# A chunked state-space scan and a feed-forward pair on one core: PSUM banks as tensors of their own, single-head outputs, dense tokens, another order of lead-in and weight decode

## The chip, the cores and the metric

The kernel runs on one core of a Trainium2 chip. The metric is device time in microseconds (us), the median of several executions; lower is better. Profiles come from one execution each. Names of engines: PE is the TensorE matmul, PEld its weight load, DVE the VectorE, ACT the ScalarE, POOL the GpSimd, SP the SyncE, whose queue issues nearly all DMAs here.

## What is computed

The reference, cut to what matters (4 batches, 8 heads, 768 tokens, head size 32, state size 16; feed-forward 256 to 2048 to 256):

```python
log_a = np.log(np.clip(a, 1e-06, 1.0))
for c in range(nc):                                   # chunks of tokens
    cum = np.cumsum(la, axis=-1)
    L = np.exp(cum[..., :, None] - cum[..., None, :]) * causal
    M = np.einsum('bhin,bhjn->bhij', Cc, Bc) * L
    y[:, :, sl] = M @ xc + (Cc @ state) * np.exp(cum)[..., None]
    state = exp(sum(la)) * state + sum_j(Bc_j xc_j * exp(cum_last - cum_j))
h = x @ w_in                                          # x: the scan's y, 3072 x 256
out = np.maximum(0.01 * h, h) @ w_out
```

The weights come in as 64-bit floats and are decoded on the chip.

## The kernel before

**Scan.** 12 chunks (`NC`) of 64 tokens (`Q`). Heads go in 4 pairs (`NG`), so 16 pairs of a head pair and a batch (`GB`). In each chunk PE does `states` (B by x into the state, 16 products), `scores` (C by B, 16), `decays` (exponents of L, 2), `outputs` (16 products of C and the old state, then 16 of the weighted scores and x) and `passed` (4). A 32-bit product is two matmuls with a weight load each. `spread_b` makes a block form of B (`bbd`) on DVE, `weigh` multiplies scores by decays on DVE, `weigh_b`, `weigh_c` and `end_decay` run on POOL, `decay_exp`, `passed_exp` and `keep_out` on ACT. Tokens lie block-diagonally in `xbd`: the two heads of a pair on 64 partitions each, with zeros beside them, so that one product of 128 by 64 serves both heads.

**Queues.** The order is written by hand, and every engine runs its instructions in that order. SP's queue carries the input chunks (`fetch_b`, `fetch_x`), the decay rows (`send_rows` to `dr`, `send_cols` to `dl`) and the raw weights (`fetch_w`). A wait is set between instructions that use the same tile.

**PSUM.** Four tiles `PS[0]` to `PS[3]` of two banks each serve the whole kernel. In the feed-forward `HB` is the two halves of `PS[0]` and of `PS[1]`, and `acc(t, m)` is half `m` of `PS[2 + t % 2]`.

**Feed-forward, first part.** Six stretches of 512 tokens (t = 0 to 5). For t = 0 and 1 there are 32 steps s: for hidden block f = s // 2 and t = s % 2, six matmuls of 128x128 by 128x512 (`products`: three for each half of the 256 inputs, since operands are split in a high and a low part) into `HB[s % 4]`; ACT makes `gh` and the activation in place, DVE the low part `gl`; two steps later (`LAG`) `ffn_out` issues six matmuls that add into `acc`. Between them run the decode jobs of the later blocks, three after each step: `dec_abs` (ACT), `dec_clamp`, `dec_shift`, `dec_sign`, `dec_low` (DVE), `dec_high` (ACT) and `dec_rest` (POOL), and for each pair of blocks `sum_weights` (POOL, ACT, POOL). In the last 24 steps `token_forms` are added.

**Feed-forward, second part.** The tokens of t = 2, 3 and then of t = 4, 5 go by a seven-product scheme: 8 blocks for each pair, 16 in all. A block is 21 matmuls into A, B, C, E (the four `HB`), of which A, B and C are written twice, and 24 matmuls of `ffn_out` by `run_out`. After A's first product ACT copies it (`act.copy(a, A)`), and DVE adds B to it. `store(t)` copies the two halves of `acc` out by ACT and DVE into `obs[m]` and sends them.

The second part begins as follows in each block:

```python
products(A, w_in(f0, 0), x(0), True, True)
act.copy(a, A)
products(B, sw(1), x(4), True, True)
dve.tensor_tensor(out=u2, in0=B, in1=a, op=ALU.add)
products(C, sw(0), x(3), True, True)
products(E, sw(2), x(5), True, True)
```

Of the kernel before, what the change touches and what calls it, by code (L numbers as in the profile page):

```python
# [45 lines left out]
def scan_ffn(ctx: ExitStack, tc: tile.TileContext, a_l, bcn_l, x_l, w_l, out_l):  # L46
# [10 lines left out]
    psum = open_pool(ctx, "psum", space=PSUM)  # L57

    PS = [psum.tile([128, 2, TS], F32, name=f"ps{i}") for i in range(4)]
# [4 lines left out]
    idle = base.tile([128, TS], BF16, name="idle")  # L64
# [67 lines left out]
    scan = ExitStack()  # L132
    cst = open_pool(scan, "cst", side="right")
# [3 lines left out]

    la = cst.tile([128, NC * GB], F32, name="la")
# [12 lines left out]
    xbd = [cst.tile([128, 2, GB * D], F32, name=f"xbd{i}") for i in range(4)]  # L151

    bcn, bbd, bnd, lts, es, cds, ss, tmps = ({} for _ in range(8))
# [12 lines left out]
    dve.memset(idle, 0.0)  # L166
    act.preload_act_table_set("natural_log_exp_and_others")
# [4 lines left out]

    sp.dma_start(la, a_l)
    fetch_b(0)
    fetch_x(0)
    keep_warm(PS[2][:, 0], WARM)

    dve.memset(later, 0.0)
    dve.memset(blk, 0.0)
    for hp in range(2):  # L180
        dve.memset(blk[64 * hp:64 * hp + 64, hp], 1.0)
    dve.memset(sign[:, :2], 1.0)
    dve.memset(sign[:, 2:], -1.0)
    pool.affine_select(
        out=later, in_=later, pattern=[[1, Q]], compare_op=ALU.is_ge, fill=-32768.0, base=0,
        channel_multiplier=-1,
    )
    pool.affine_select(
        out=upto, in_=blk, pattern=[[64, 2], [1, Q]], compare_op=ALU.is_ge, fill=0.0, base=0,
        channel_multiplier=-1,  # L190
    )
    pool.affine_select(
        out=after, in_=blk, pattern=[[-64, 2], [-1, Q]], compare_op=ALU.is_gt, fill=0.0, base=0,
        channel_multiplier=1,
    )
# [8 lines left out]
    dve.tensor_copy(  # L204
        dl[:64, :, 0], upto[:64, 0].unsqueeze(1).to_broadcast([64, NC, Q])
    )
    dve.tensor_copy(
        dl[:64, :, 1], upto[:64, 0].unsqueeze(1).to_broadcast([64, NC, Q])
    )
    dve.tensor_copy(dr[:64, 0], later.unsqueeze(1).to_broadcast([64, GB, Q]))  # L210
# [3 lines left out]
    act.copy(  # L214
        dl[64:KD, 0], sign[64:KD, :2].unsqueeze(2).to_broadcast([KD - 64, 2, Q])
    )
    dve.tensor_copy(dl[64:KD, 1:], dl[64:KD, :1].to_broadcast([KD - 64, NC - 1, 2, Q]))
    dve.tensor_tensor(out=seen, in0=upto[:, 0], in1=upto[:, 1], op=ALU.add)

    halves = [slice(0, GB // 2), slice(GB // 2, GB)]  # L220
    for h in range(2):
        pe.matmul(
            PS[0][:, h].rearrange("p (g i) -> p g i", i=Q), lhsT=dl[:64, 0],
            rhs=later.unsqueeze(1).to_broadcast([64, GB // 2, Q]), start=True, stop=True,
        )
# [4 lines left out]
    def fill_reach(h, eng):  # L230
        eng.tensor_tensor(
            out=reach[:, halves[h]],
            in0=la[:, halves[h]].unsqueeze(2).to_broadcast([128, GB // 2, Q]),
            in1=seen.unsqueeze(1).to_broadcast([128, GB // 2, Q]), op=ALU.mult,
        )

    prow = PS[3][:, 0].rearrange("p (a i) -> p a i", i=2 * Q)
    pcol = PS[3][:, 1, :NC * GB]
    flat = upto.rearrange("p h i -> p (h i)")
    pe.matmul(prow[:, 0], lhsT=la[:, :128], rhs=flat, start=True, stop=True)  # L240
    pe.matmul(prow[:64, 1], lhsT=la[:, 128:], rhs=flat, start=True, stop=True)
    fill_reach(0, pool)
    fill_reach(1, dve)
# [24 lines left out]
    def fill_slots(lo, hi):  # L268
        dve.tensor_copy(dr[:KD, lo:hi], dr[:KD, :1].to_broadcast([KD, hi - lo, GB, Q]))

    fill_slots(1, 4)
    split(0, 128)
    send_rows(1, 4, (0, 1, 2, 3, 4, 5), sp)
    send_cols(1)
    pe.matmul(
        pcol, lhsT=after.rearrange("p h i -> p (h i)"), rhs=la, start=True, stop=True
    )
    for h in range(2):
        pe.matmul(
            PS[0][:, h].rearrange("p (g i) -> p g i", i=Q),  # L280
            lhsT=after.rearrange("p h i -> p (h i)"), rhs=reach[:, halves[h]],
            start=False, stop=True, skip_group_check=True,
        )
# [39 lines left out]
    for i in range(4):  # L323
        for hp in range(2):
            p = slice(64 * hp, 64 * hp + 64)
            (dve if i == 0 else pool).memset(xbd[i][p, 1 - hp], 0.0)
    spread_b(0)

    def split_x(c):
        return xbd[c % 4].rearrange("p h (d g) -> p (h d) g", g=GB)  # L330

    def scores(c):
        for b in range(NB):
            for g in range(NG):
                r = slice(32 * g, 32 * g + 32)
                pe.matmul(
                    PS[1 + g // 2][:, g % 2, b * Q:(b + 1) * Q], lhsT=bbd[c][r, b].rearrange("p h i -> p (h i)"),
                    rhs=bcn[c][r, CT + b * Q:CT + (b + 1) * Q], start=True, stop=True,
                )

    def weigh(c, half):
        m = lts[c][:, 8 * half:8 * half + 8].rearrange("p (g b) i -> p g (b i)", g=2)
        dve.tensor_tensor(out=m, in0=PS[1 + half][:, :, :CT], in1=m, op=ALU.mult)

    zspace = PS[1][:, 1, CT:]
    espace = PS[3][:, 1, CT:]

    def states(c):
        x = split_x(c)
        for b in range(NB):  # L350
            for g in range(NG):
                gb = g * NB + b
                pe.matmul(
                    zspace[32 * g:32 * g + 32, b * 64:(b + 1) * 64], lhsT=bnd[c][:, gb].rearrange("p h n -> p (h n)"),
                    rhs=x[:, :, gb], start=True, stop=True, skip_group_check=True,
                )

    def keep_state(c):
# [49 lines left out]
    def outputs(c):  # L408
        x, mt = split_x(c), lts[c]

        def place(g, b):
            o = 64 * (g % 2)
            return PS[3][o:o + 64, g // 2, b * Q:(b + 1) * Q]

        if c:
            for b in range(NB):
                for g in range(NG):
                    r = slice(32 * g, 32 * g + 32)
                    pe.matmul(
                        place(g, b), lhsT=ss[c - 1][r, b * 64:(b + 1) * 64],  # L420
# [3 lines left out]
        for b in range(NB):  # L424
            for g in range(NG):
                gb = g * NB + b
                pe.matmul(
                    place(g, b), lhsT=x[:, :, gb], rhs=mt[:, gb], start=(c == 0 and b == 0),
                    stop=True, skip_group_check=True,
                )  # L430

    def keep_out(c):
        t, o = divmod(c, 2)
        cols = slice(o * CT, (o + 1) * CT)
        y = PS[3][:, :, :CT]
# [5 lines left out]
    def low_out(c):  # L441
        t, o = divmod(c, 2)
        cols = slice(o * CT, (o + 1) * CT)
        if t < 2:
            dve.tensor_tensor(
                out=xl[t][:, :, cols], in0=PS[3][:, :, :CT], in1=xh[t][:, :, cols],
# [3 lines left out]
    work = collections.deque()  # L450
    for f in range(EARLY_F):
        for g in (dec_abs, dec_clamp, dec_shift, dec_sign, dec_low):
            work.append((g, f))
        work.append((dec_rest, f))

    def background(n):
        for _ in range(n):
            if work:
                g, f = work.popleft()
                g(f)  # L460
                if g is dec_low:
                    dec_high(f)

    fetch_b(1)
    fetch_x(1)
    send_cols(2)
    for c in range(NC + 1):
        if 1 <= c < NC:
            states(c - 1)
        if c < NC:  # L470
            scores(c)
        if 1 <= c < NC:
            keep_state(c - 1)
        if c < NC:
            weigh(c, 0)
            weigh(c, 1)
            if c < NC - 1:
                weigh_b(c)
        if c + 1 < NC:
            decays(c + 1)  # L480
            decay_exp(c + 1)
        if c >= 1:
            outputs(c - 1)
        if c + 1 < NC:
            passed(c + 1)
        if c >= 1:
# [22 lines left out]
        if c >= 4:  # L509
            background(2)  # L510
    background(99)
# [12 lines left out]
    HB = [PS[0][:, 0], PS[0][:, 1], PS[1][:, 0], PS[1][:, 1]]  # L524

    def acc(t, m):
        return PS[2 + t % 2][:, m]
# [29 lines left out]
    def store(t):  # L557
        for m in range(2):
            ob = obs[m]
# [3 lines left out]
    obs = [mid.tile([128, TS], F32, name=f"ob{m}") for m in range(2)]  # L563


    def sum_weights(p):
# [3 lines left out]
        for o, x, y, op in (  # L570
# [39 lines left out]
    jobs = collections.deque()  # L610
    summed = 0
    for f in range(EARLY_F, NF):
# [152 lines left out]
```

## Time and profile before

| | |
|---|---|
| median of 3 runs | 425.88 us (425.29 to 426.62) |
| the profiled execution | 425.0 us |
| its span, first to last instruction | 423.3 us |
| PE busy, share of the span | 352.7 us, 83% |
| DVE, ACT, POOL busy | 210.2, 177.2, 86.0 us |
| mean granted TensorE clock | 0.945 of full speed |

The profile is of one core. A busy PE means that a matmul is in its pipeline, and not that it runs at its peak; matmuls overlap, so the step from one matmul's start to the next tells more than its duration. Idle time that is shown ahead of an instruction names the engine or transfer that ended it.

### The profile page before, as it was taken

To read this page: it belongs to the slowest core of one execution; us is meant where nothing else is said; L and a number is where in the kernel's file an instruction comes from. 1 tells how busy PE (TensorE), PEld (TensorE's weight loads), DVE (VectorE), ACT (ScalarE), POOL (GpSimd) and SP (SyncE) were. 2 spreads that over 40 slices of the span, in tenths; PEclk is the share of its full clock that TensorE was granted. 3 is DMA by queue.
4 is the path that set the end of the run, shared out by engine and by line. 5 is a ranking of instruction groups with operands and counts; after the bars stand their busy time and mean duration, and the time that the engine had idled before them with its cause. 6 is when DMAs were issued, how large, how long until landed. Compare 5 with 4: busy or idle time off the path is not lost.

```text
span 423.3 us, 6595 instructions
## 1 busy us (share of the span) xinstructions
PE 352.7 (83%) x2662; PEld 269.8 (64%) x2662; DVE 210.2 (50%) x352; ACT 177.2 (42%) x309; POOL 86.0 (20%) x114
## 2 busy tenths in 40 slices
PE   5849999976979787676669699999999799999994
PEld 2437888755757555454446477777777677777783
DVE  7624656433644545433333556666555555455551
ACT  2303433334544553433223555455444344444441
POOL 5422444413253442423123010000000000000000
PEclk8868999999998898979889899999999999999998
DMA  2256483103112111110000200000000200000002
GB/s 72 69 138 211 131 260 114 53 0 101 50 50 98 53 50 50 50 50 2 0 0 0 99 2 0 1 2 0 0 2 0 100 2 0 1 2 0 0 2 99
DMA packets 9902, 20.19 MB, mean 48 GB/s; under 512 B 3088, under 2 KB 3216, under 8 KB 9872
## 3 DMA queue, kind: packets, MB, share of 16 engines
q1 hardware_dynamic: 9872, 19.77, 14.3%
q8 instruction: 21, 0.34, 0.3%
q14 instruction: 9, 0.07, 0.0%
HBM read 16.35 MB, written 3.15 MB: 46 GB/s over the span
## 4 chain that ended last, share of the span: by engine, by line
PE 49%; ACT 11%; DVE 6%; POOL 5%; issue 4%; DMA 1%; ACTq 0%; DVEq 0%
PE ps L532 49%; POOL wtmp L576 2%; POOL wlb L127 2%; ACT gh L629 2%; ACT tmp L693 2%; ACT ps L630 2%; DVE gl L631 2%; DMA out_l<-ob 1%; DVE w L117 1%; ACT whb L124 1%; DVE w L111 1%; ACT gh L676 1%; ACT ob L560 1%; ACT w L97 1%; POOL wla L127 1%
## 5 line engine op out<-in xcount | busy, mean ns | idle before, releaser
L631 DVE TENSOR_TENSOR gl<-ps,gh 128x512 fp32r<-128x512 f32 x32 | 22.1, 690 | 78.3 <-ACT ps L630 78.3
L676 ACT ACTIVATE gh<-tmp 128x512 fp32r<-128x512 f32 x48 | 30.1, 628 | 67.0 <-DVE tmp L700 63.9
L532 PE MATMUL ps<-gh,whb 128*128 128x512 f32 x120 | 49.0, 408 | 0.0
L532 PE MATMUL ps<-gh,wlb 128*128 128x512 f32 x120 | 48.9, 408 | 0.0
L532 PE MATMUL ps<-gl,whb 128*128 128x512 f32 x120 | 48.5, 404 | 0.0
L678 DVE TENSOR_TENSOR gl<-tmp,gh 128x512 fp32r<-128x512 f32 x48 | 33.2, 692 | 20.6 <-ACT tmp L677 20.6
L532 PE MATMUL ps<-oph,wsh 128*128 128x512 f32 x64 | 27.6, 432 | 14.3 <-ACT tmp L693 14.3
L629 ACT ACTIVATE gh<-ps 128x512 fp32r<-128x512 f32 x32 | 19.0, 594 | 44.4 <-PE ps L532 43.3
L532 PE MATMUL ps<-xh,whb 128*128 128x512 f32 x40 | 18.3, 459 | 21.2 <-DVE gl L631 12.3
L677 ACT ACTIVATE tmp<-tmp 128x512 f32<-128x512 f32 x48 | 30.4, 632 | 1.5
L695 DVE TENSOR_TENSOR tmp<-ps,tmp 128x512 f32<-128x512 f32 x16 | 11.1, 692 | 37.8 <-PE ps L532 37.8
L532 PE MATMUL ps<-gh,wla 128*128 128x512 f32 x72 | 29.0, 402 | 0.0
L532 PE MATMUL ps<-gh,wha 128*128 128x512 f32 x72 | 28.8, 400 | 0.0
L532 PE MATMUL ps<-gl,wha 128*128 128x512 f32 x72 | 28.8, 400 | 0.0
L532 PEld LDWEIGHTS ps<-gh,whb 128*128 128x128 f32 x120 | 23.9, 199 | 5.7
L532 PEld LDWEIGHTS ps<-oph,wsh 128*128 128x128 f32 x64 | 12.4, 194 | 23.5 <-ACT tmp L693 21.2
L532 PEld LDWEIGHTS ps<-gh,wlb 128*128 128x128 f32 x120 | 23.8, 198 | 5.6
L532 PEld LDWEIGHTS ps<-gl,whb 128*128 128x128 f32 x120 | 23.7, 197 | 5.4
L532 PEld LDWEIGHTS ps<-xh,whb 128*128 128x128 f32 x40 | 8.4, 211 | 28.5 <-DVE gl L631 15.8
L532 PE MATMUL ps<-opl,wsh 128*128 128x512 f32 x64 | 25.7, 402 | 0.0
L532 PE MATMUL ps<-oph,wsl 128*128 128x512 f32 x64 | 25.7, 401 | 0.0
L127 POOL TENSOR_TENSOR wlb<-w,whb 128x512 fp32r<-128x512 f32 x10 | 12.7, 1275 | 63.5 <-ACT whb L124 63.5
(136 smaller groups left out, 722.7 us busy)
## 6 DMA issues: line engine op xcount, KB each, us to landing
raw<-w_l SPq DMA_DIRECT2D x16, 512.0 KB, 3.3
bcn<-bcn_l SPq DMA_DIRECT2D x12, 384.0 KB, 4.2
xbd<-x_l SPq DMA_DIRECT2D x24, 128.0 KB, 3.9
out_l<-ob SPq DMA_DIRECT2D x12, 256.0 KB, 2.0
dr<-parts SPq DMA_DIRECT2D x12, 8.0 KB, 1.9
dl<-parts SPq DMA_DIRECT2D x11, 12.0 KB, 3.8
la<-a_l SPq DMA_DIRECT2D x1, 96.0 KB, 1.9
dr<-parts SPq DMA_DIRECT2D x6, 6.0 KB, 1.8
```

The costliest lines, as they stand in the source:

```text
L97: act.activation(w32(f), raws[f][..., 1].bitcast(F32), AF.Abs)
L127: (eng or dve).tensor_tensor(out=weight(1, f), in0=w32(f), in1=weight(0, f), op=ALU.subtract)
L532: pe.matmul(space, lhsT=w, rhs=x, start=start and i == 0, stop=stop and i == 2, skip_group_check=again,)
L576: pool.tensor_tensor(out=o, in0=x, in1=y, op=op)
L629: act.activation(gh, hp, AF.Prelu, alpha=0.01)
L630: act.activation(hp, hp, AF.Prelu, alpha=0.01)
L631: dve.tensor_tensor(out=gl, in0=hp, in1=gh, op=ALU.subtract)
L676: act.activation(gh, v, AF.Prelu, alpha=0.01)
L677: act.activation(v, v, AF.Prelu, alpha=0.01)
L678: return g, lambda: dve.tensor_tensor(out=gl, in0=v, in1=gh, op=ALU.subtract)
L693: act.copy(a, A)
L695: dve.tensor_tensor(out=u2, in0=B, in1=a, op=ALU.add)
```

## The change

Six things are done.

1. In the feed-forward each of the eight PSUM banks is a tile of its own: `HB` four tiles, `ACC` four tiles. In the scan there are still four tiles of two banks (`pd`, `pa`, `pb`, `py`); `espace` moves from the tile of the outputs to that of the scores.
2. Tokens are dense (`xs`, one DMA for each chunk in place of two, and no zeros to set). `states` has 32 moving columns in place of 64, and `keep_state` does the block form by two DVE instructions with a mask. The second half of `outputs` is 32 products of 64 rows by 32 columns, one for each head and batch, in place of 16 of 128 by 64.
3. In the chunk loop `passed` and `passed_exp` go one chunk earlier.
4. The lead-in is in another order: `send_rows(1, 2)` ahead of the rest, two of its six DMAs on ACT's queue, fewer rows of `dl` to fill, four more warming matmuls.
5. The decode is placed step by step: `duty` in the scan, `plan` in the first part of the feed-forward, where block f's jobs lie in steps 2f-5 to 2f-1, and the forms come from step 4 on.
6. `obs` has four buffers, the fourth in `wtmp`.

```diff
-    PS = [psum.tile([128, 2, TS], F32, name=f"ps{i}") for i in range(4)]
+    pd, pa, pb, py = (psum.tile([128, 2, TS], F32, name=n) for n in ("pd", "pa", "pb", "py"))
...
-            for hp in range(2):
-                p = slice(64 * hp, 64 * hp + 64)
-                sp.dma_start(xbd[c % 4][p, hp], x_l[c, p])
+            xs[c] = pin.tile([128, GB, D], F32, name="xs")
+            sp.dma_start(xs[c].rearrange("p g d -> p (g d)"), x_l[c])
...
-    fill_slots(1, 4)
+    fill_reach(0)
     split(0, 128)
-    send_rows(1, 4, (0, 1, 2, 3, 4, 5), sp)
+    send_rows(1, 2, range(0, 4), sp)
+    send_rows(1, 2, range(4, 6), act)
     send_cols(1)
+    fill_reach(1)
+    fill_slots(2, 4)
...
         for b in range(NB):
-            for g in range(NG):
+            for h in range(NH):
+                g, hp = divmod(h, 2)
+                r = slice(64 * hp, 64 * hp + 64)
+                o = 32 * (h % 4)
                 gb = g * NB + b
                 pe.matmul(
-                    place(g, b), lhsT=x[:, :, gb], rhs=mt[:, gb], start=(c == 0 and b == 0),
-                    stop=True, skip_group_check=True,
+                    py[o:o + 32, h // 4, b * Q:(b + 1) * Q], lhsT=xs[c][r, gb], rhs=mt[r, gb],
+                    start=(c == 0 and b == 0), stop=True, skip_group_check=True,
                 )
...
     fetch_b(1)
     fetch_x(1)
+    send_rows(2, 4, range(6), sp)
     send_cols(2)
     for c in range(NC + 1):
+        if c + 1 < NC:
+            passed(c + 1)
...
         if c == 0:
             split(1, 64)
             fill_slots(4, 8)
+        if c == 1:
             send_rows(4, 8, range(6), sp)
...
-    HB = [PS[0][:, 0], PS[0][:, 1], PS[1][:, 0], PS[1][:, 1]]
+    HB = [psum.tile([128, TS], F32, name=f"h{i}") for i in range(4)]
+    ACC = [psum.tile([128, TS], F32, name=f"o{i}") for i in range(4)]
...
-            ob = obs[m]
+            ob = obs[t % 2 * 2 + m]
...
+    for f in range(NF):
+        o = 2 * (f - EARLY_F)
+        if f >= EARLY_F:
+            at(o - 1, dec_abs, f)
+            at(o, dec_clamp, f)
+            at(o, dec_shift, f)
+            at(o + 1, dec_sign, f)
+            at(o + 1, dec_low, f)
+            at(o + 2, dec_high, f)
+            at(o + 3, dec_rest, f, pool)
```

PE in the first part of the feed-forward, block f = 6, before: the end of one step's `ffn_out` and the products of t = 1 (`ps_61` is `PS[0]`, of which t = 0 has the other half).

```order
L532 MATMUL ps_63<-gh_1315,wha 128x512
L532 MATMUL ps_63<-gh_1315,wla 128x512
L532 MATMUL ps_63<-gl_1316,wha 128x512
L532 MATMUL ps_61<-xh_82,whb 128x512 [waits DVE_49]
L532 MATMUL ps_61<-xh_82,wlb 128x512
```

The same place now (`h_1529` is the second `HB`, `o_1533` and `o_1534` are `ACC`):

```order
L526 MATMUL o_1533<-gl_1519,wha 128x512
L526 MATMUL h_1529<-xh_74,whb 128x512
L526 MATMUL h_1529<-xh_74,wlb 128x512
L526 MATMUL h_1529<-xl_76,whb 128x512
L526 MATMUL h_1529<-xh_74,whb 128x512
L526 MATMUL h_1529<-xh_74,wlb 128x512
L526 MATMUL h_1529<-xl_76,whb 128x512
L526 MATMUL o_1534<-gh_1520,wha 128x512 [waits Activation_49]
```

The order is the same; the wait for DVE ahead of t = 1's products is gone, and the sums into `ACC` wait for their own `gh` and `gl`, which belong to two steps earlier.

PE in the second part, the start of a block, before (A and B are the halves of `ps_61`, C and E of `ps_62`):

```order
L532 MATMUL ps_61<-oph_1309,whb 128x512 [waits DVE_49]
L532 MATMUL ps_61<-oph_1309,wlb 128x512
L532 MATMUL ps_61<-opl_1310,whb 128x512
L532 MATMUL ps_61<-oph_1309,wsh 128x512 [waits Activation_49]
L532 MATMUL ps_61<-oph_1309,wsl 128x512
```

The same place now, from B's first product to A's second:

```order
L526 MATMUL h_1529<-oph_1512,wsh 128x512
L526 MATMUL h_1529<-oph_1512,wsl 128x512
L526 MATMUL h_1529<-opl_1513,wsh 128x512
L526 MATMUL h_1530<-oph_1512,wsh 128x512 [waits DVE_49]
L526 MATMUL h_1530<-oph_1512,wsl 128x512
L526 MATMUL h_1530<-opl_1513,wsh 128x512
L526 MATMUL h_1531<-oph_1512,wsh 128x512
L526 MATMUL h_1531<-oph_1512,wsl 128x512
L526 MATMUL h_1531<-opl_1513,wsh 128x512
L526 MATMUL h_1529<-oph_1512,whb 128x512 [waits DVE_49]
L526 MATMUL h_1529<-oph_1512,wlb 128x512
L526 MATMUL h_1529<-opl_1513,whb 128x512
```

B's first product no longer waits for ACT's copy of A; that wait now stands ahead of A's second product, which follows these rows, and B's second product waits for the DVE sum that has read B.

SP's queue in the lead-in, before (`dr` rows of slots 1 to 3, then of slots 4 to 7; `bcn` are the chunks of B and C):

```order
L256 DMA dr<-parts_109 1x48x64 x6
L263 DMA dl<-parts_109 48x1x128
L158 DMA bcn<-bcn_l 128x768
L164 DMA xbd_114<-x_l 64x512 x2
L263 DMA dl<-parts_109 48x1x128
L256 DMA dr<-parts_109 1x64x64 x6
L158 DMA bcn<-bcn_l 128x768
```

The same queue now:

```order
L251 DMA dr<-parts_109 1x16x64 x4
L258 DMA dl<-parts_109 48x1x128
L156 DMA bcn<-bcn_l 128x768
L161 DMA xs<-x_l 128x512
L251 DMA dr<-parts_109 1x32x64 x6
L258 DMA dl<-parts_109 48x1x128
L156 DMA bcn<-bcn_l 128x768
L161 DMA xs<-x_l 128x512
L258 DMA dl<-parts_109 48x1x128
L251 DMA dr<-parts_109 1x64x64 x6
L156 DMA bcn<-bcn_l 128x768
```

The input of chunk 2 (the third `bcn`) stood behind the six rows of slots 4 to 7, which wait for a split and a fill on DVE; it now stands ahead of them, behind six rows of slots 2 and 3, and it is chunk 3's input that follows the rows of slots 4 to 7.

## Rows read from the trace of the kernel before

**Rows 1.** Busy time by stretch: us, PE, PEld, DVE, ACT, POOL, clock, DMA

```profile
35.78:78.82 43.04, 43.04 (x1076) 35.48 (x1073) 24.90 (x53) 17.29 (x28) 19.84 (x24) 1.00 0.54 168
...
86.79:227.10 140.31, 103.91 (x375) 76.20 (x374) 59.10 (x95) 58.89 (x108) 47.10 (x56) 0.91 0.12 42
227.10:416.10 189.00, 173.81 (x727) 136.05 (x727) 103.98 (x156) 89.64 (x156) 3.18 (x3) 0.99 0.03 12
416.10:423.30 7.20, 1.36 (x6) 0.76 (x4) 1.38 (x2) 1.17 (x2) 0.00 (x0) 0.82 0.40 146
```

**Rows 2.** Waits from 86.79 to 227.1 us: total us, times, longest us

```profile
PE ps L532 <- DVE gl L631: 22.4, 14, 3.5
...
PE ps L532 <- ACT whb L124: 8.9, 5, 2.5
...
PE ps L532 <- POOL wlb L127: 5.1, 6, 0.9
```

**Rows 3.** Waits of the whole span, same columns

```profile
PE ps L532 <- ACT tmp L693: 14.3, 16, 2.6
```

**Rows 4.** Timeline of one step of the first part: start us, us, engine, line, operation

```profile
147.71 0.40 PE L532 MATMUL ps<-xh,whb 128*128 128x512 f32 x1
...
149.37 0.60 ACT L629 ACTIVATE gh<-ps 128x512 fp32r<-128x512 f32 x1 [2.10 <-PE ps L532]
...
149.87 0.59 ACT L630 ACTIVATE ps<-ps 128x512 f32<-128x512 f32 x1
...
150.27 0.40 PE L532 MATMUL ps<-gl,whb 128*128 128x512 f32 x1
150.49 0.69 DVE L631 TENSOR_TENSOR gl<-ps,gh 128x512 fp32r<-128x512 f32 x1 [1.69 <-ACT ps L630]
...
151.24 0.50 PE L532 MATMUL ps<-xh,whb 128*128 128x512 f32 x1 [0.57 <-DVE gl L631]
```

**Rows 5.** Timeline of the second part: a block's copy, its products, a stall between blocks

```profile
236.52 0.49 PE L532 MATMUL ps<-oph,wha 128*128 128x512 f32 x1 [0.87 <-DVE gl L678]
...
275.09 0.58 ACT L693 COPY tmp<-ps 128x512 f32<-128x512 f32 x1 [1.41 <-PE ps L532]
...
275.73 0.50 PE L532 MATMUL ps<-oph,wsh 128*128 128x512 f32 x1 [0.68 <-ACT tmp L693]
...
276.07 0.40 PE L532 MATMUL ps<-oph,wsl 128*128 128x512 f32 x1
...
285.93 0.40 PE L532 MATMUL ps<-opl,whb 128*128 128x512 f32 x1
```

**Rows 6.** Timeline of PE in one chunk of the scan

```profile
46.54 1.07 PE L353 MATMUL ps<-xbd,bnd 128*32 128x64 f32 x32
...
49.13 0.69 PE L419 MATMUL ps<-cd,ss 32*64 32x64 f32 x32
...
49.76 2.00 PE L427 MATMUL ps<-lt,xbd 128*64 128x64 f32 x32
...
51.92 0.30 PE L353 MATMUL ps<-xbd,bnd 128*32 128x64 f32 x4
```

**Rows 7.** Timeline of the lead-in and chunks 2 and 3

```profile
6.93 1.75 DVE L269 COPY dr<-dr 118x3072 bf16<-118x3072 bf16 x1
...
21.00 3.73 SPq L256 DMA_DIRECT2D dr<-parts  x6
...
24.77 0.58 SPq L158 DMA_DIRECT2D bcn<-bcn_l  x1
...
29.69 1.99 PE L336 MATMUL ps<-bcn,bbd 32*128 32x64 f32 x32 [6.28 <-DVE bbd L301]
...
36.78 1.12 PE L336 MATMUL ps<-bcn,bbd 32*128 32x64 f32 x32
```

**Rows 8.** Timeline of the end

```profile
417.06 0.40 PE L532 MATMUL ps<-gl,whb 128*128 128x512 f32 x1
...
419.58 0.69 DVE L560 COPY ob<-ps 128x512 f32<-128x512 f32 x1 [2.17 <-ACT ob L560]
```

**Rows 9.** Group by line, 35.78 to 78.82 us: busy us, mean ns of one

```profile
L427 PE MATMUL ps<-lt,xbd 128*64 128x64 f32 x256 | 16.0, 278 | 0.0
```

More of the change, by code (lines that the diff above doesn't have):

```diff
@@ L132, in scan_ffn @@
     scan = ExitStack()
+    psum = open_pool(scan, "psum", space=PSUM)
+    pd, pa, pb, py = (psum.tile([128, 2, TS], F32, name=n) for n in ("pd", "pa", "pb", "py"))
     cst = open_pool(scan, "cst", side="right")
@@ L136, in scan_ffn @@
     p3 = open_pool(scan, "p3", bufs=3, side="right")
+    idle = cst.tile([128, TS], BF16, name="idle")
     la = cst.tile([128, NC * GB], F32, name="la")
@@ L150, in scan_ffn @@
     reach = cst.tile([128, GB, Q], F32, name="reach")
-    xbd = [cst.tile([128, 2, GB * D], F32, name=f"xbd{i}") for i in range(4)]
-    bcn, bbd, bnd, lts, es, cds, ss, tmps = ({} for _ in range(8))
+    bcn, xs, bbd, bnd, lts, es, cds, ss, tmps = ({} for _ in range(9))
     def fetch_b(c):
@@ L181, in scan_ffn @@
         dve.memset(blk[64 * hp:64 * hp + 64, hp], 1.0)
[L182 to L195, printed above, removed]
+    dve.memset(later, 0.0)
+    keep_warm(pa[:, 0], WARM)
     pool.affine_select(
@@ L228, in scan_ffn, with fill_reach @@
     act.activation(la, la, AF.Ln)
-    def fill_reach(h, eng):
-        eng.tensor_tensor(
+    dve.tensor_tensor(out=seen, in0=upto[:, 0], in1=upto[:, 1], op=ALU.add)
+    fill_slots(1, 2)
+    prow = py[:, 0].rearrange("p (a i) -> p a i", i=2 * Q)
+    pcol = pb[:, 0, :NC * GB]
+    pe.matmul(prow[:, 0], lhsT=la[:, :128], rhs=flat_upto, start=True, stop=True)
+    pe.matmul(prow[:64, 1], lhsT=la[:, 128:], rhs=flat_upto, start=True, stop=True)
+    keep_warm(pa[:, 0], 4)
+    def fill_reach(h):
+        dve.tensor_tensor(
             out=reach[:, halves[h]],
@@ L445, in low_out @@
             dve.tensor_tensor(
-                out=xl[t][:, :, cols], in0=PS[3][:, :, :CT], in1=xh[t][:, :, cols],
+                out=xl[t][:, :, cols], in0=py[:, :, :CT], in1=xh[t][:, :, cols],
                 op=ALU.subtract,
             )
-    work = collections.deque()
+    duty = collections.defaultdict(list)
     for f in range(EARLY_F):
[L452 to L462, printed above, removed]
+        o = 4 + 4 * f
+        duty[o].append((dec_abs, f))
+        duty[o + 1] += [(dec_clamp, f), (dec_shift, f)]
+        duty[o + 2].append((dec_sign, f))
+        duty[o + 3].append((dec_low, f))
+        duty[o + 4].append((dec_high, f))
+        duty[o + 5].append((dec_rest, f))
     fetch_b(1)
     fetch_x(1)
+    send_rows(2, 4, range(6), sp)
     send_cols(2)
     for c in range(NC + 1):
+        if c + 1 < NC:
+            passed(c + 1)
         if 1 <= c < NC:
@@ L471, in scan_ffn @@
             scores(c)
+        if c + 1 < NC:
+            passed_exp(c + 1)
+            decays(c + 1)
+            decay_exp(c + 1)
         if 1 <= c < NC:
@@ L558, in store @@
         for m in range(2):
-            ob = obs[m]
+            ob = obs[t % 2 * 2 + m]
             (act.copy if m == 0 else dve.tensor_copy)(ob, acc(t, m))
             sp.dma_start(out_l[m, :, t * TS:(t + 1) * TS], ob)
-    obs = [mid.tile([128, TS], F32, name=f"ob{m}") for m in range(2)]
+    obs = [mid.tile([128, TS], F32, name=f"ob{m}") for m in range(3)]
+    obs.append(wtmp.rearrange("p a f -> p (a f)"))
     def sum_weights(p):
@@ L608, in token_forms, with at @@
         return todo
[L610 to L619 removed]
+    forms = collections.deque(token_forms(2, *ops[0]))
+    plan = collections.defaultdict(list)
+    def at(s, g, *args):
+        plan[s].append((g, args))
+    for f in range(NF):
[8 more added lines that the diff above has]
+            at(o + 3, dec_rest, f, pool)
+        if f % 2:
+            o = max(o, -1)
+            at(o + 2, sum_weights, f // 2)
+            at(o + 3, sum_high, f // 2)
+            at(o + 4, sum_low, f // 2)
+    for g, args in plan[-1]:
+        g(*args)
     LAG = 2
@@ L625, in scan_ffn @@
         hp = HB[s % 4]
+        for g, args in plan[s]:
+            g(*args)
         for k in range(2):
@@ L632, in scan_ffn @@
         queue.append((f, t, g))
-        for _ in range(3):
-            if jobs:
-                jobs.popleft()()
-        if s >= 2 * NF - 24 and forms:
+        if s >= 4 and forms:
             forms.popleft()()
@@ L639, in scan_ffn @@
             ffn_out(*queue.popleft())
-    while jobs:
-        jobs.popleft()()
-    while forms:
-        forms.popleft()()
+    assert not forms
     early.close()
```

166 lines of the change are left out of this document (78 added, 88 removed).

## The prediction

> **What bounds the kernel now.** I read the table of stretches first, then the waits, then the timeline at the places that they name. By the table of stretches [rows 1] the span has a lead-in, a scan of equal chunks, the first part of the feed-forward (140.31 us), its second part (189.00) and an end (7.20). In the middle of the scan PE is busy for all of 43.04 us: there the number and kind of PE's instructions set the time. In the feed-forward the work is the same kind of matmul throughout, so the test is its step. While nothing stops it, the step is (150.27 - 147.71) / 11 = 0.233 us in the first part [rows 4] and (285.93 - 276.07) / 43 = 0.229 in the second [rows 5]. By the code the first part has 32 x 6 + 30 x 6 = 372 matmuls, 86.6 us at that step against 140.31; the second has 727 in its stretch [rows 1], 166.7 us against 189.00. So about 54 and 22 us there are not matmul steps but waits, and a lower clock behind them (0.91 of full speed in the first part, 1.00 in the scan [rows 1]). Who is waited for: in the first part 22.4 us for DVE's `gl`, 8.9 for `dec_high` and 5.1 for `dec_rest` [rows 2]; in the second 14.3 us for ACT's copy of A [rows 3], 16 times. The other engines do not bound it: DVE, ACT and POOL are busy 59.10, 58.89 and 47.10 of the first part's 140.31 us [rows 1].
>
> **The first part.** PE waits for `gl` ahead of t = 1's products [rows 4]: they begin at 151.24, after ACT's two instructions and DVE's one, though their operands are long there. What they wait for is DVE's reading of the other half of the same PSUM tile. As tiles of their own the two halves have no such wait, and the new order shows none. What is late next is the true need: the sums into `acc`, which want `gh` and `gl` of two steps before. From the end of a step's products (149.37, when `gh` starts) to the end of `gl` (150.49 + 0.69 = 151.18) are 1.8 us; between those products and their own sums PE has 24 matmuls, 5.6 us. So 3.8 us of delay are hidden. The weights come next. In the plan `dec_rest` is placed one step ahead of its use. Its predecessors lie one step apart each, a step is 12 x 0.233 = 2.8 us, and each engine reaches its job at a step's head once the `gl` or the activation of the step before is done. I follow `dec_high`: behind the activation of step 2f-3, which is some 2.6 us after that step's start; then `dec_rest`, which ends about 2 us into step 2f-2. It is needed at step 2f, some 3 us later. I therefore take both weight waits to go. ACT, DVE and POOL have the same jobs in less time: 59.10 / 87.6 = 67% for DVE and for ACT, 54% for POOL. One us is left for the start. New time 86.6 + 1.0 = 87.6: **-52.7 us**. This takes the clock back to 1.00, as it is in the scan where PE has no gaps [rows 1]. Bounds: all of it, 86.6; or, with the weight waits of 8.9 + 5.1 kept and a clock share of some 6 us for them, 107.6.
>
> **The second part.** B's first product waits for the copy of A, its neighbour in the tile: A's last product ends at 275.09, the copy takes 0.58, B starts at 275.73 [rows 5]. Now it starts at once. Next in line is B's second product, which needs DVE's sum of B and the copy. PE works on C and E meanwhile, 6 x 0.229 = 1.37 us; the sum takes 0.69 once B is out and the copy (0.58) runs beside B's three matmuls (0.69). About 0.5 us remain, with DVE busy 103.98 of now some 169 us [rows 1]. The later waits (C's second product for its DVE sum, the next block's A for `gl`) lie behind 6 and 24 matmuls. Two blocks of the 16 also hold the `store` copies and have less cover; a stall there was 0.87 us [rows 5], and I leave 2.0 us for both. The buffers `obs`, four of them, take away the waits of the second `store` for the first one's transfer. New time 166.7 + 2.0 = 168.7: **-20.3 us**, between -22.3 (no stall) and -12 (half of the 16 waits come back as waits for the sum).
>
> **The end.** The last matmul ends at 417.06 + 0.40. Then the second store's copy by DVE waits until 419.58 for a buffer that is still being sent, and 3.0 us after its end (420.27) the span is over [rows 8]. With a fourth buffer the copy starts at once: 417.46 + 0.7 + 3.0 = 421.2, **-2.1 us**.
>
> **The lead-in.** In chunk 2 PE stands 6.28 us for `bbd`, since `bcn` of that chunk is issued only at 24.77, behind six row DMAs of 3.73 us that begin at 21.00 [rows 7]. That input now stands ahead of them: -6.3. What moves back is chunk 3's input, behind those same six, and six more row DMAs lie ahead of chunk 2's. The cold stretch after the wait goes with it: from `scores` of chunk 2 to those of chunk 3 are 7.09 us against a period of 51.92 - 46.54 = 5.38 [rows 6, 7], -1.7. Fewer slots are filled ahead of the split (one in place of the three that took 1.75 us [rows 7]), so rows leave earlier, but `passed` now needs them ahead of the first `scores`, and fills, warming matmuls and ACT's two DMAs stand in between; I take -1.5. Sum **-9.5 us**. Bounds: -7.1, if chunk 3's input is as late as chunk 2's was (its `scores` then start at 29.69), and -11.
>
> **The chunks.** From 35.78 to 78.82 are eight periods of 5.38 us, PE full [rows 1, 6]. `states` keeps 32 instructions with half the columns: 1.07 us now, and no less than the quickest step in a chunk, 32 x 0.69 / 32 = 0.69; I take 0.87. `outputs` has 64 instructions in place of 32 (2.00 us). At the step of the old state's products (32 rows by 64 columns, 0.69 / 32 = 0.0216) they take 1.38, at that of `states` (0.0334) 2.14. The head's place ties its rows to its columns, so four places are used in turn, as in `states`: I take the latter row. Sum 0.87 + 2.14 - 1.07 - 2.00 = -0.1 a chunk, **-0.8** for eight; bounds -1.0 and +0.14 a chunk. `keep_state` has two instructions for one, and `passed` now waits for `weigh`: PE has over 3 us of `decays` and `outputs` behind `scores`, DVE some 2 us of work. DVE's 24.90 of 43.04 us [rows 1] leave room.
>
> **Sum.** -52.7 - 20.3 - 2.1 - 9.5 - 0.8 = -85.4. The profiled execution took 425.0 us (span 423.3); 425.0 - 85.4 = 339.6. It lies 0.9 below the median of the runs shown, 425.88, so the forecast for the median is 340.5 us.
>
> **Rivals.** (1) The weights come too late, one step being too little: the waits of 14.0 us and some 6 of clock stay, 360. For it: `dec_high` and `dec_rest` sit in the queues of engines that also wait for PE. Against it: the 3 us worked out above.
>
> (2) A single-head product costs as much as a product of two heads did: 64 x 2.00 / 32 = 4.0 us, +1.9 a chunk against my sum, +22 over 12: 363. Against it: `states`, with columns as narrow, steps twice as fast.
>
> (3) Neighbouring single-head products use different rows and write one bank. If those could not overlap, each would take a place's whole time, 2 x 2.00 / 32 = 0.125, or 8.0 us a chunk: +5.9 x 12 = +70, 411. The row speaks against it: the old state's products also alternate rows, two of four neighbours write one bank, and they step by 0.0216 us [rows 6]. The Trainium skill, TensorEngine Tiling (Array Packing), section Restrictions and Gotchas, says that different row tiles cannot access the same PSUM bank at the same time; by that rule this rival would be the forecast, and the trace so far does not agree.
>
> (4) Slower than before: the single-head products do not overlap at all, and each takes what one lasts, 0.278 us [rows 9]: 17.8 us a chunk, +15.7 x 12 = +188, 528. It decides from 2.14 + 85.4 / 12 = 9.3 us a chunk, 0.145 for each product. `states` steps by a quarter of that.
>
> That the split does not take the waits away is excluded by the new order, in which neither stands.
>
> **How the numbers follow.** Forecast 0.82, rival 1 0.10, rival 2 0.04, rival 3 0.02, rival 4 0.02. Low end: chunks at their lower bound (-10 us) and no stall in the feed-forward (-3) give 327; I take 328. High end 361: it takes in rival 1, or half of each upper bound (10 us of weights, 4 of sums, 2 of lead-in) and some more; rivals 2 to 4 stay outside. A measurement of this kernel tells 0.3% from no change, and only rival 4 is not faster: faster 0.975, within 0.3% 0.005, slower 0.02.
>
> **What would show it.** In the profile of the changed kernel: no wait of PE for `gl` or the copy of A; the first part near 88 us with the clock at 1.00; blocks of the second part at 45 x 0.23 = 10.4 us without a gap; `outputs` at 2.8 us with the old state's products, and a period near 5.3; no wait for `bbd` in chunk 2. I am wrong if PE waits for `dec_rest` at each new block, if `outputs` takes over 4 us, or if chunk 3 has chunk 2's wait.

## The result, and the profile after

The changed kernel takes 344.08 us (median of 4, 342.86 to 348.69) against 426.25 for the kernel before: a ratio of 0.806, 95% interval 0.802 to 0.810. The forecast was 340.5. The profiled execution took 342.86 us, its span is 341.1, its mean clock 0.975. Some executions of a kernel are slower as a whole, at a lower mean clock (here the 348.69, 0.936 against 0.965 to 0.975): the medians below count them, the ratios leave them out, and the profiles of two runs below, shared banks (384.62 us) and rows first (355.41 us), are of such executions.

The page of the changed kernel: busy time by engine, and the queue that brings instructions (packets, MB, share of 16 DMA engines):

```profile
PE 318.4 (93%) x3050; PEld 251.6 (74%) x3050; DVE 232.0 (68%) x362; ACT 179.5 (53%) x309; POOL 89.3 (26%) x107
...
q8 instruction: 24, 0.39, 0.4%
```

Its waits of PE in the whole span (total us, times, longest us; "issue" is idle time in which PE waits for nothing that the profile shows):

```profile
PE pb L389 <- DMA dr<-parts: 5.0, 2, 3.7
PE pb L323 <- issue: 2.9, 2, 2.5
PE pa L323 <- DVE bbd L295: 2.0, 4, 0.6
PE pa L339 <- issue: 1.8, 1, 1.8
PE py L422 <- issue: 1.6, 2, 1.1
PE h L526 <- POOL wla L123: 1.4, 1, 1.4
...
PE h L526 <- DVE tmp L702: 1.3, 1, 1.3
PE py L410 <- issue: 1.2, 2, 0.8
```

Its stretches (columns as in [rows 1]): the eight chunks, the feed-forward's two parts and the end:

```profile
26.52:71.07 44.55, 36.36 (x1329) 28.11 (x1325) 31.39 (x59) 17.47 (x27) 19.86 (x25) 0.89 0.53 171
77.93:167.10 89.17, 87.71 (x382) 70.37 (x377) 74.94 (x96) 59.26 (x109) 56.67 (x56) 1.00 0.19 69
167.10:337.50 170.40, 169.07 (x730) 136.60 (x728) 104.08 (x156) 90.83 (x157) 2.58 (x2) 1.00 0.04 14
337.50:341.10 3.60, 0.03 (x1) 0.00 (x0) 0.69 (x1) 0.00 (x0) 0.00 (x0) 1.00 0.62 229
```

The same two parts of the kernel before, cut at the same instructions (the second begins with B's first product):

```profile
86.79:228.50 141.71, 104.63 (x378) 76.45 (x376) 59.54 (x95) 59.48 (x109) 47.75 (x56) 0.92 0.12 41
228.50:417.46 188.96, 174.45 (x729) 136.56 (x729) 104.23 (x156) 89.64 (x155) 2.53 (x2) 0.99 0.03 12
```

The waits of [rows 2, 3] are gone but for 1.4 us (for `wla`), a new one of 1.3 us stands in the second part, and PE fills the feed-forward. In the eight chunks the picture is turned round: PE was busy for all of 43.04 us [rows 1], and is now for 36.36 of 44.55. PE's timeline there, with three stalls, a chunk that has one and a quick one:

```profile
39.15 0.26 PE L339 MATMUL pa<-xs,bnd 128*32 128x32 f32 x4 [1.84 <-issue]
...
47.73 0.87 PE L422 MATMUL py<-lt,xs 64*32 64x64 f32 x46 [1.10 <-issue]
...
52.95 0.46 PE L339 MATMUL pa<-xs,bnd 128*32 128x32 f32 x32
...
56.91 0.47 PE L323 MATMUL pb<-bcn,bbd 32*128 32x64 f32 x2 [2.46 <-issue]
...
60.84 1.89 PE L422 MATMUL py<-lt,xs 64*32 64x64 f32 x64
...
62.89 0.46 PE L339 MATMUL pa<-xs,bnd 128*32 128x32 f32 x32
...
64.87 0.69 PE L410 MATMUL py<-cd,ss 32*64 32x64 f32 x32
65.49 1.10 PE L422 MATMUL py<-lt,xs 64*32 64x64 f32 x64
...
66.75 0.46 PE L339 MATMUL pa<-xs,bnd 128*32 128x32 f32 x32
```

The quick period is 66.75 - 62.89 = 3.86 us; the one before it 9.94, with a stall named issue of 2.46 us, and slower products behind it (1.89 us in place of 1.10; the granted clock is 0.50 from 56.9 to 61 us). Eight quick periods would be 30.9 us. Of the 13.7 us above that, PE stands still for 8.2 (44.55 - 36.36; 5.9 are named issue, 2.0 are for `bbd`), and the other 5.5 are products that are slower at the lower clock.

| term | predicted | measured |
|---|---|---|
| first part | -52.7 | 141.71 to 89.17: -52.5 |
| second part | -20.3 | 188.96 to 170.40: -18.6 |
| end | -2.1 | 5.84 to 3.60: -2.2 |
| up to chunk 3's `states` | -9.5 | 35.78 to 26.52: -9.3 |
| eight chunks | -0.8 | 43.04 to 44.55: +1.5 |
| last chunk | 0 | 7.97 to 6.86: -1.1 |

They add up to -82.2, the difference of the spans. Two questions are left: which of the edits did the first part's 52.5 us, and why products that are quicker than forecast gain nothing in the eight chunks.

### The profile page after: what moved, and what is told of

Read it like the earlier page. It is cut to its first block, busy times and chain, and to the rows that moved or that the text cites. A ratio compares the mean times of both kernels' runs of the same rounds, so it can differ in the third digit from the quotient of the medians.

```text
span 341.1 us, 7379 instructions
## 1 busy us (share of the span) xinstructions
PE 318.4 (93%) x3050; PEld 251.6 (74%) x3050; DVE 232.0 (68%) x362; ACT 179.5 (53%) x309; POOL 89.3 (26%) x107
## 4 chain that ended last, share of the span: by engine, by line
PE 66%; DVE 14%; issue 5%; SPq 5%; ACT 4%; DMA 3%; POOL 3%; ACTq 0%; DVEq 0%; POOLq 0%
PE o L526 31%; PE h L526 27%; SPq L251 4%; DMA bcn<-bcn_l 3%; DVE w L107 3%; DVE gl L644 2%; PE py L422 2%; DVE opl L585 2%; DVE bbd L295 2%; PE py L410 1%; POOL wtmp L571 1%; PE pa L323 1%; DVE w L113 1%; DVE w L96 1%; PE pa L170 1%
## 5 line engine op out<-in xcount | busy, mean ns | idle before, releaser
L685 DVE TENSOR_TENSOR gl<-tmp,gh 128x512 fp32r<-128x512 f32 x48 | 33.2, 692 | 21.2 <-ACT tmp L684 21.2
L526 PE MATMUL o<-gl,whb 128*128 128x512 f32 x120 | 47.1, 393 | 0.0
L526 PE MATMUL o<-gh,wlb 128*128 128x512 f32 x120 | 47.1, 393 | 0.0
L526 PE MATMUL o<-gh,whb 128*128 128x512 f32 x120 | 46.9, 391 | 0.0
L526 PE MATMUL o<-gh,wla 128*128 128x512 f32 x72 | 28.5, 395 | 0.0
L526 PE MATMUL o<-gl,wha 128*128 128x512 f32 x72 | 28.4, 395 | 0.0
L526 PE MATMUL o<-gh,wha 128*128 128x512 f32 x72 | 28.4, 394 | 0.0
L526 PEld LDWEIGHTS o<-gh,whb 128*128 128x128 f32 x120 | 22.6, 188 | 5.3
L526 PE MATMUL h<-oph,wsl 128*128 128x512 f32 x64 | 25.2, 394 | 0.0
L526 PE MATMUL h<-opl,wsh 128*128 128x512 f32 x64 | 25.2, 394 | 0.0
L526 PE MATMUL h<-oph,wsh 128*128 128x512 f32 x64 | 25.2, 393 | 0.0
```

Source lines behind the costliest of these rows:

```text
L526: pe.matmul(space, lhsT=w, rhs=x, start=start and i == 0, stop=stop and i == 2, skip_group_check=again,)
L685: return g, lambda: dve.tensor_tensor(out=gl, in0=v, in1=gh, op=ALU.subtract)
```

## Experiments on the feed-forward

**Banks alone, on the kernel before.**

```diff
-    HB = [PS[0][:, 0], PS[0][:, 1], PS[1][:, 0], PS[1][:, 1]]
+    HB = [psum.tile([128, TS], F32, name=f"h{i}") for i in range(4)]
+    ACC = [psum.tile([128, TS], F32, name=f"o{i}") for i in range(4)]
```

> The kernel before, with only the eight PSUM banks of the feed-forward as tiles of their own; the decode jobs stay three after each step, the forms late, obs of two buffers, scan and lead-in as before. Theory (the waits for DVE's gl and for ACT's copy of A are the shared tiles, and the weights are a cost of their own): the first part goes from 140.3 to about 107 us, since waits for dec_high and dec_rest of 14 us and some 6 us of lower clock stay, and the second from 189 to about 171: 425.9 - 33 - 18 = 375 us. Rival 1 (the weights only look late because everything is): first part 88, 356 us in all. Rival 2 (the jobs, three a step, cannot keep up with PE's shorter steps, and a weight wait takes the place of each gl wait): first part 125 or more, 392 us.

Measured: 399.91 us. The first part takes 132.7, the second 173.2:

```profile
87.00:219.70 132.70, 107.03 (x379) 80.77 (x376) 59.29 (x95) 58.49 (x108) 47.98 (x56) 0.86 0.13 44
219.70:392.90 173.20, 169.44 (x730) 136.46 (x729) 104.14 (x157) 90.26 (x156) 2.59 (x2) 1.00 0.04 14
```

The theory was wrong for the first part, and rival 2 near: the waits for `gl` are gone, and PE waits 25.7 us for weights in place of 14.0.

**Three jobs a step again, in the changed kernel.**

```diff
-        for g, args in plan[s]:
-            g(*args)
...
+        for _ in range(3):
+            if jobs:
+                jobs.popleft()()
```

> The changed kernel with the decode jobs of the first part as before, three after each step, and the forms in the last 24 steps; banks stay tiles of their own. Theory (three a step is too late for the weights): waits of PE for dec_high and dec_rest of about 14 us and some 6 us of lower clock: 364 us. Rival (with the gl wait gone the queues of ACT and POOL are no longer held and the jobs come in time): within 3 us of the changed kernel, 346 us.

Measured: 386.45 us, 42.4 above the changed kernel, twice what the theory expected. First part 131.0, second 170.4:

```profile
77.90:208.90 131.00, 103.85 (x384) 78.09 (x377) 60.05 (x96) 58.92 (x109) 47.45 (x57) 0.90 0.15 48
```

Its waits for weights (there are 2.0 us more at the earliest blocks, 27.2 in all):

```profile
PE h L526 <- ACT whb L120: 18.1, 8, 3.6
PE h L526 <- POOL wlb L123: 7.1, 9, 0.9
```

Its timeline where a late block begins:

```profile
186.29 0.69 DVE L631 TENSOR_TENSOR gl<-h,gh 128x512 fp32r<-128x512 f32 x1 [2.10 <-ACT h L630]
186.90 0.68 DVE L107 SCALAR_TENSOR_TENSOR w<-raw,w 128x512 uint32<-128x512 uint32 x1
187.61 0.69 DVE L113 SCALAR_TENSOR_TENSOR w<-raw,w 128x512 uint32<-128x512 uint32 x1
188.34 0.62 ACT L120 CAST whb<-w 128x512 fp32r<-128x512 f32 x1 [2.08 <-DVE w L113]
189.01 0.49 PE L526 MATMUL h<-xh,whb 128*128 128x512 f32 x1 [2.56 <-ACT whb L120]
...
190.36 0.56 PE L526 MATMUL h<-xh,wlb 128*128 128x512 f32 x1 [0.85 <-POOL wlb L123]
```

DVE is idle for 2.10 us and then takes `gl`, because the decode stands behind `gl` in its queue; only then come two decode jobs, ACT's and POOL's, and PE stands for 3.4 us. In the kernel before PE stood for `gl` itself meanwhile, and the same lateness showed as 14 us [rows 2]. The plan puts the jobs ahead of `gl`. Waits are not the whole price: for the same products PE is busy 103.85 us here and 87.71 in the changed kernel, 16 us of slower products at a clock of 0.90 in place of 1.00. This run also has the token forms late again; what their place alone does was not tried.

**Shared banks, in the changed kernel.**

```diff
+    PS = [psum.tile([128, 2, TS], F32, name=f"ps{i}") for i in range(4)]
+    HB = [PS[0][:, 0], PS[0][:, 1], PS[1][:, 0], PS[1][:, 1]]
```

> The changed kernel with the banks of the feed-forward in four shared tiles of two again, nothing else undone. Theory (the shared tiles cost a wait for gl at each step of t = 1 and a wait for the copy at each block): first part from 88.6 to about 118 us (22.4 of gl waits and some 7 of clock), second part from 171 to about 189: 344 + 30 + 18 = 392 us. Rival (the plan alone would have taken most of it, since gl comes earlier when DVE is less crowded): gl waits under 8 us, 370 us.

Measured: 377.65 us, 33.6 above. First part 107.4, second 185.4, with these waits, one in each part:

```profile
85.90:193.30 107.40, 93.59 (x380) 70.57 (x375) 74.69 (x96) 59.83 (x110) 51.03 (x56) 0.98 0.16 54
193.30:378.70 185.40, 173.04 (x729) 135.62 (x729) 104.15 (x156) 89.76 (x156) 2.54 (x2) 1.00 0.03 12
PE ps L526 <- DVE gl L644: 13.2, 16, 2.0
PE ps L526 <- ACT tmp L700: 12.1, 16, 1.9
```

The waits for `gl` lie between what the theory (22.4) and the rival (under 8) took. The two parts together are 33.2 us longer than in the changed kernel, close to the difference of the medians.

| first part, us | three jobs a step | plan |
|---|---|---|
| shared banks | 141.7 (before) | 107.4 |
| own banks | 132.7 (131.0 with the new scan) | 89.2 (after) |

So the plan is worth 34 us without the banks, the banks 9 without the plan, and the two together 52.5. In the second part the banks do most of it (185.4 against 170.4, 15.0 of 18.6).

**Two output buffers.**

```diff
-            ob = obs[t % 2 * 2 + m]
+            ob = obs[m]
```

> The changed kernel with two output buffers in place of four. Theory: the second store's copy by DVE waits again for a buffer that is being sent, +2.1 us at the end, and the stores inside the second part hold DVE and ACT for some 2 us where PE waits for them: 348 us. Rival (the stores have cover by 24 matmuls): only the end, 346 us. Rival 2: 344 us, if the end is set by something else.

Measured: 349.73 us. The second part is 173.2 in place of 170.4 (as it is with the banks alone, which also has two buffers), and the end 1.5 us longer; the rest of the 5.65 us is scan, which differs between executions. The theory holds.

## Experiments on the scan

**Rows of slots 4 to 7 ahead of chunk 2's input.**

```diff
             fill_slots(4, 8)
-        if c == 1:
             send_rows(4, 8, range(6), sp)
```

> The changed kernel with the rows of slots 4 to 7 sent after chunk 0 again, ahead of chunk 2's input. Theory (the term of -6.3 us in the sum is this place): chunk 2's bcn is issued some 6 us later, PE waits about 5 to 6 us for bbd in chunk 2 and is cold after it, chunk 3 loses its small wait of 0.6: 350 us. Rival (the scan has other late inputs that hide it): within 2 us of the changed kernel, 344 to 346 us.

Measured: 348.71 us, +4.6 (ratios 0.816 and 0.806); PE waits 4.4 us for `bbd` in chunk 2, the longest of these three:

```profile
PE pa L323 <- DVE bbd L295: 5.4, 3, 4.4
```

The theory holds in the main: the wait is there, shorter than the 5 to 6 us expected.

**Block-diagonal tokens again.**

```diff
-            for h in range(NH):
+            for g in range(NG):
...
-                    py[o:o + 32, h // 4, b * Q:(b + 1) * Q], lhsT=xs[c][r, gb], rhs=mt[r, gb],
+                    py[o:o + 64, g // 2, b * Q:(b + 1) * Q], lhsT=x[:, :, gb], rhs=mt[:, gb],
```

> The changed kernel with block-diagonal tokens again: states with 64 columns, one keep_state instruction, outputs of 16 products of 128 by 64, two token transfers a chunk, four buffers for tokens. Theory (the quicker products of the change are given back by stalls of PE in the scan, which come from instructions and inputs that arrive late at the quicker pace): PE is full again at 5.4 us a chunk, its idle time named issue is under 2 us in the scan (7.5 us in the changed kernel), and the time is within 2 us of the changed kernel, 343 to 346 us. Rival 1 (dense tokens and single heads pay by their instructions, 1.5 us a chunk): 344 + 16 = 360 us. Rival 2 (they cost more than they bring): 338 us.

Measured: 345.10 us, all runs within 345.03 and 345.68. Its stretch of eight chunks:

```profile
29.68:72.49 42.81, 42.81 (x1072) 35.38 (x1068) 29.49 (x51) 17.63 (x27) 18.01 (x23) 1.00 0.60 167
```

The instruction queue on its page:

```profile
q8 instruction: 21, 0.34, 0.4%
```

No stall of PE named issue is left, PE is full, the clock is 1.00. With longer products the eight chunks take 1.7 us less than in the changed kernel. What dense tokens bring lies beside them: in this run chunk 3's `states` start at 29.68 in place of 26.52, 3.2 us later, and the last chunk takes 7.97 in place of 6.86. On the whole that is about 1 us, no more than runs of the changed kernel vary.

**Loads taken away from the chunks.** First the raw weights alone, which go to the lead-in, then the inputs too.

```diff
-        if c in (2, 4, 6):
-            fetch_w(c // 2 - 1)
```

> The changed kernel with the first three raw weight blocks (1.5 MB) fetched in the lead-in on ACT's queue, behind the first rows, and those of blocks 3 and 4 after the scan; no raw weights are fetched in the chunks. Theory A (PE's stalls named issue are instruction refills that come late while the raw weights fill the 16 DMA engines): stalls named issue from 22 to 78 us fall from 7.5 us to under 3 us, the clock of those stretches stays at 1.00, the lead-in loses 2 us: 338 to 341 us. Theory B (refills are late at this pace whatever the other transfers do): stalls of 6 to 8 us remain, 344 to 347 us.

Measured: 346.04 us; stalls of 5.0 us, between what the theories expected, and a lead-in 2.4 us longer (chunk 3's `states` at 28.88). This one decides nothing.

```diff
+        if 3 <= c < NC:
+            bcn[c] = bcn[c % 3]
```

> The same, and from chunk 3 on no inputs are fetched: the chunks use the B, C and tokens of chunks 0 to 2 again (the fetches of nine chunks are left out, so the values differ). Theory A: no late inputs, no refill beside loads, stalls named issue under 1 us, period 3.9 us from chunk 4 on, feed-forward starts some 12 us earlier: 330 to 333 us. Theory B: a stall of about 1 us every 512 instructions remains, 5 to 8 us in all: 338 us.

Measured: 340.77 us. Its stretch of eight chunks:

```profile
29.44:66.72 37.28, 32.16 (x1329) 24.86 (x1325) 31.90 (x60) 17.61 (x27) 18.74 (x24) 1.00 0.08 23
```

Two of PE's waits there, from 25 to 76 us:

```profile
PE pa L330 <- DVE bbd L302: 3.7, 6, 0.6
PE pb L330 <- issue: 1.1, 1, 1.1
```

With a DMA share of 0.08 in place of 0.53 the longest stall is 1.1 us, all of them 2.5 in place of 7.5, and the period is 37.28 / 8 = 4.66 in place of 5.57. Neither theory holds in size: the stalls lie between A's (under 1 us) and B's (5 to 8), and the feed-forward starts at 75.86 us, 2.1 earlier and not 12, after a lead-in that is 2.9 us longer (29.44). The period is not 3.9: DVE has 31.90 us of work there and PE waits 3.7 us for its `bbd`, so DVE looks like the next bound; no run shows it alone.

A part of DVE's work was made longer by the change itself. In the kernel before, POOL is idle while DVE makes `bbd`; in the new order POOL's `weigh_c` and `weigh_b` run beside it, and the same two instructions take 1.55 us in place of 0.61 (first line before, the others the changed kernel):

```profile
39.55 0.61 DVE L301 TENSOR_SCALAR bbd<-bcn,odd 128x256 f32<-128x256 f32 x2
...
66.22 1.55 DVE L295 TENSOR_SCALAR bbd<-bcn,odd 128x256 f32<-128x256 f32 x2
66.52 1.10 POOL L371 TENSOR_TENSOR bnd<-bcn,erev 128x512 f32<-128x512 f32 x1
```

The run with `bbd` on ACT, below, takes it off DVE at no gain; none keeps POOL away from it, so what that would bring is not shown.

What the stalls are: the instruction queue counts 24 packets of 16 KB, for 2 x 3050 instructions of PE, 254 a packet; before it was 21 for 2 x 2662, again 254. The stalls at 39.15, 47.73 and 56.91 us stand 254 and 253 matmuls apart, each with a weight load: twice 254 and 253 instructions. A smaller one, 0.46 us at 34.99, stands 128 matmuls ahead of the first, half as far. So the stalls fit the ends of blocks of PE's instructions, and come when 332 instructions a chunk are used up at the quick pace while transfers are heavy. The Trainium skill, Runtime: NRT & Kernel Launch, section Instruction fetch mechanics, says that instructions come in blocks of 256 and that crossing one is mostly hidden; the count agrees, the stalls of up to 2.5 us do not. That the fetch waits behind the data in the DMA engines is inferred from this; no row shows it.

**Trying to keep the gain.** Inputs three chunks ahead and raw weights in the lead-in; then `bbd` on ACT as well; then, instead, ten more warming matmuls.

```diff
-        fetch_b(c + 2)
-        fetch_x(c + 2)
+        fetch_b(c + 3)
+        fetch_x(c + 3)
```

> The changed kernel with four buffers for inputs in place of three, inputs three chunks ahead instead of two (those of chunk 1 at the very start), two of the six row transfers of slots 2 and 3 on ACT's queue, and the first three raw weight blocks behind chunk 3's input in the lead-in. Theory (late transfers, and instruction refills behind them, give back the scan's gain): the wait for rows of slots 2 and 3 falls from 3.7 to about 2 us, no wait for bcn, stalls named issue under 4 us: 338 to 340 us. Rival (the scan is held by DVE, which has 4.2 us of work a chunk while POOL slows its bbd): 342 to 344 us.

> The same, and the block form of B is made by ACT, ahead of its copy of the outputs, in place of DVE. Theory (DVE's two bbd instructions take 1.55 us a chunk when POOL works beside them, and PE waits for them at the quicker pace): no wait of PE for bbd, period about 4.3 us: 334 to 337 us. Rival (ACT comes to bbd later than DVE did, or PE is held by the instruction refills alone): no better than the version without it, 338 to 342 us.

> The version with earlier inputs (block form of B on DVE), with six more warming matmuls of 128x512 between chunk 0's exponents and its row products and four more after the first half of chunk 0's weighing. In the version without them PE's wait of 1.5 us at 9 us was followed by a granted clock of 0.50 from 11 to 62 us, although PE was busy for all of 16 to 70 us. Theory (that stretch, not waits, holds it): the clock stays at 1.00 up to 22 us and beyond, the period is near 4.3 us, the feed-forward starts at 68 to 72 us: 333 to 337 us. Rival (the clock falls in the scan anyway, at a stall or because of what the small products are): a clock of 0.5 to 0.6 in several stretches of 22 to 62 us, 341 to 345 us.

Measured: 344.60, 348.23 and 346.38 us, ratios to the kernel before of 0.810, 0.809 and 0.817, where the changed kernel has 0.806: none is better. All three theories missed. The second has executions of 343.74 to 351.90 us; its `bbd` from ACT is late too (1.8 us of waits), and its clock is 0.50 from 20 to 30 us. The first has hardly a wait left, and this instead (stretches of its scan):

```profile
11.10:20.32 9.22, 8.43 (x172) 5.80 (x165) 7.62 (x15) 3.01 (x5) 4.04 (x5) 0.50 0.66 223
20.32:60.64 40.32, 40.32 (x1000) 31.15 (x996) 24.52 (x45) 12.64 (x20) 14.30 (x19) 0.50 0.47 137
```

PE is busy throughout at half the clock, 40.32 / 6 = 6.72 us a chunk. Its four runs lie between 342.18 (mean clock 0.963) and 347.19 us (0.921, the one shown). The early inputs are not needed for this: the profile of the run with shared banks, whose scan is the changed kernel's, has a clock of 0.52 from 27.45 to 61.19 us with PE busy for 33.23 of 33.74. Why the clock does not come back there stays open. With more warming the clock is 1.00 up to 22.8 us, and then:

```profile
18.00:22.80 4.80, 2.90 (x103) 2.11 (x102) 4.11 (x8) 1.43 (x3) 2.65 (x4) 1.00 1.02 378
22.80:26.40 3.60, 0.81 (x50) 0.64 (x47) 2.22 (x4) 0.57 (x1) 2.08 (x3) 0.95 0.47 103
26.40:33.00 6.60, 6.60 (x169) 5.08 (x173) 3.54 (x7) 1.99 (x3) 2.09 (x3) 0.51 0.80 243
```

A burst of raw weights at 378 GB/s, a stall of 2.8 us, and a clock of 0.51 behind it: the rival. Last, the same lead-in with block-diagonal tokens:

```diff
+    keep_warm(pa[:, 0], 6)
...
+            if c == 0:
+                keep_warm(pa[:, 0], 4)
```

> The changed kernel with block-diagonal tokens again (as in the run with those alone, 345.1 us), and in the lead-in: chunk 1's input fetched at the very start, two of the six row transfers of slots 2 and 3 on ACT's queue, and the ten warming matmuls of the last version. Raw weights, buffers and the order of fetches in the chunks as in the changed kernel. Theory (at 268 PE instructions a chunk instead of 332 over 5.4 us no refill is late, so what is gained in the lead-in is kept): the wait for rows of slots 2 and 3 falls from 4.2 to about 1.5 us, the granted clock stays at 1.00 where it was 0.50 from 13 to 25 us (some 4 us of time), no stall named issue: 345 - 2.7 - 3.5 = 339 us, with all runs within 1 us. Rival (another late input, or stalls, give it back as in the quicker scan): 343 to 345 us.

Measured: 342.87 us, ratio to the kernel before 0.802 (0.799 to 0.805); its interval overlaps that of the changed kernel, so it is not shown to be better. The waits for rows and the cold lead-in are gone, and a late `bbd` of 1.3 us in chunk 3 with a low clock behind it (0.66 from 30 to 35 us) gives part of it back. The theory's 339 us, with all runs within 1 us, did not come: they lie between 340.54 and 347.03.

## Why the prediction was right, and where its steps were not

- **First part**: right in size (-52.7 and -52.5). Wrong was the bound of 107.6 us "with the weight waits kept", and rival 1 with it (20 us): kept, the waits are 27.2 us in place of 14.0 and the lower clock costs some 16 in place of 6, and the first part is 131.0. The waits were read from a trace in which PE stood elsewhere meanwhile.
- **Second part**: the mechanism held; 1.7 us were over-estimated. Of the 2.0 us left for stalls, 1.3 came (in the second block, ahead of B's second product, for DVE's sum: the wait that was named as next in line); but PE's 729 products take 169.1 us, 0.232 each in place of 0.229.
- **End**: as worked out.
- **Lead-in**: right in its sum by two errors. Chunk 2, from its `states` to the next, went from 13.45 to 4.63 us, -8.8 where -8.0 was taken. The "earlier lead-in" of -1.5 gave 0.4: chunk 1's `states` start at 16.33, before at 16.10, and chunk 2's at 21.89, before at 22.33, since `passed` waits 3.74 us for rows of slots 2 and 3, which was named and not priced.
- **Chunks**: the mis-sized term. `states` takes 0.46 us, not 0.87, and lies below the bound of 0.69; the single-head products take 1.10, not 2.14, 0.017 an instruction. The bound came from the quickest step in the trace, and nothing there said that no step could be quicker than that. Rivals 2 to 4 fall. The prediction had no term for what feeds PE at a period of 3.86 us: stalls, late `bbd` and the low clock behind them cost 13.7 us, where the quicker products would have brought 12.2 (8 x 1.52). That -0.8 and +1.5 lie so near is luck.
- Neighbouring single-head products alternate rows 0 to 63 and 64 to 127, four in a row write one bank, and a matmul follows the last by 0.017 us, where rival 3 took 0.125. The Trainium skill, TensorEngine Tiling (Array Packing), section Restrictions and Gotchas, says that different row tiles cannot access the same PSUM bank at the same time; the trace does not agree.

## What to carry over

Waits that hide one another are not a sum: the wait that is removed uncovers the lateness behind it, so try each edit alone before crediting it. Here decode work for a later step belonged ahead of the low-part instruction in an engine's queue, not behind it. Before making small PE instructions quicker, ask whether their refills, their inputs and the next engine keep up; a longer instruction that keeps PE full can be worth as much.

## What was not expected of the hardware

- Products of 128 rows by 32 columns step by 0.014 us (32 moving columns) and of 64 by 32 by 0.017 (64 moving columns), about half of the 0.033 that the nearest row of before suggested.
- PE stalled for up to 2.8 us, at places that fit the ends of instruction blocks, at 11.6 ns an instruction (3.86 us / 332) with transfers of 171 GB/s beside it on the mean of the eight chunks and 378 ahead of the longest stall; at 5.38 / 268 = 20 ns the scan shows no stall named issue.
- The granted clock stayed at 0.50, the lower of its two levels, for 40 us of chunks in which PE was busy all the time with small products.
